# First MLP of blocks 7 and 8 as one pair with seven products, blocks 1 to 6 ordered by the list scheduler

## The chip, the core and the metric

The kernel runs on one core of one Trainium2 chip. Five engines take their instructions each from its own queue, in order: TensorE (PE; its weight loads are listed as PEld), VectorE (DVE), ScalarE (ACT), GpSimd (POOL) and SyncE (SP). Almost all DMAs are issued by SP, a few by ACT. The metric is the device time of one execution in microseconds (us), lower is better.

## The reference

A linear attention is followed by two MLPs over the same 4608 rows. All inputs are float32.

```python
# q, k, v: (8, 8, 576, 64); w_in: (512, 2048); w_out: (2048, 512), for each MLP
q_s = softmax(q, axis=-1);  k_s = softmax(k, axis=2)      # each with its maximum subtracted
kv  = einsum('bhsd,bhse->bhde', k_s, v)
x   = einsum('bhsd,bhde->bhse', q_s, kv)   # then (batch, row, heads*64) -> (4608, 512)
h = x @ w_in;  x = (h * clip(h + 3, 0, 6) / 6) @ w_out    # first MLP
h = x @ w2_in; out = (h / (1 + exp(-h))) @ w2_out         # second MLP
```

## The kernel before

**Tiling.** The 4608 rows are nine blocks of 512 rows (block 0 to 8). A value of float32 is held as two parts, an upper one (the value cast to fp32r) and a lower one (what the cast lost), and each product of two such values is three matmuls: upper by upper, upper by lower, lower by upper. Every large matmul is 128x128 by 128x512.

**A block of an MLP, the plain way.** It has 16 steps f, one for each 128 columns of the hidden layer. `mm1` (L493) makes h of a step by 12 matmuls into one of two PSUM banks `h`. The gate follows: ACT makes r (`relu`, L506), DVE multiplies (`times`, L513), ACT casts the upper part of g (`upper`, L521), DVE makes the lower part (`lower`, L524). `mm2` (L563) adds the step to four PSUM banks y0 to y3 by 12 matmuls. The order written out by hand is mm1 of a step, then mm2 of the step before. After the 16th step, `finish` copies y0 to y3 out, two on DVE and two on ACT, and stores them to DRAM (`yd`). That makes 384 matmuls for a block.

**A pair of blocks by seven products.** `second_mlp` takes two blocks at once. The rows of the pair and the weights are each cut in quarters, and seven products of sums of quarters stand in for eight (Strassen and Winograd). `inner` (L998) is the first matmul of the MLP and `outer` (L1151) the second, with 336 matmuls each: 672 for a pair. `PAIR` names the operands: A11 ... S4 are parts of the weights, B11 ... T4 parts of the rows. The weight parts lie ready made in DRAM (`ws`) and come back by way of a ring of six buffers of 512 KB (`fetch`, L884); two parts lie in one buffer. The row parts of the next pair are made while a pair runs (`x_ahead`, `xd`).

**Stages.** Block 0 of the first MLP is ordered by a list scheduler (`Plan`: jobs with an engine, a duration, a key, what they wait for, and buffers taken and given back). Blocks 1 to 8 of the first MLP run the plain way in a loop written by hand, in which each step also holds a share of the attention of a later block (`k_max` ... `x_mm`, one unit for each pair of heads, 36 units in all, `begin` says at which step a unit starts) and of the weight parts of the second MLP (`Parts`: 16 jobs, each converts two raw rows of weights, makes four sums on POOL, splits them on ACT and DVE through a buffer `sp`, and stores them to `ws` by SP). The attention's q goes through DRAM to be transposed (`q_store`, `q_load`, issued by ACT). In block 8 the row parts of the pair (1, 2) are made (`first_operands`). Then the second MLP runs on the pairs (1, 2), (3, 4), (5, 6), (7, 8), and at last on block 0 the plain way. The transposes back to rows (`turn`, L1191) of a pair run in the pair after it.

**How an instruction waits.** Each engine takes its queue in order; an instruction whose data or buffer isn't there holds up all behind it on that engine, SP's DMAs included.

Of the kernel before, what the change touches and what calls it, by code (L numbers as in the profile page):

```python
# [9 lines left out]
F32 = mybir.dt.float32  # L10
# [8 lines left out]
P = 128  # L19
# [9 lines left out]
def efficient_attention_then_two_mlps(  # L29
# [23 lines left out]
    KVS = NP + 1  # L53

# [48 lines left out]
    class Conv:  # L103
# [68 lines left out]

    class Parts:

        def __init__(self, i, o):
# [8 lines left out]

        def sums(self):
            at = {}
            for c, names in zip(self.conv, self.names):
                for h, name in enumerate(names):
                    at[name] = c.a[:, h * HALF : (h + 1) * HALF]
            self.s = raw.tile([P, 4, HALF], F32, tag="raw", name="ws_sum")  # L190
            for n in range(4):
                at[f"S{n + 1}"] = self.s[:, n]
            for to, x, y, op in (
                ("S1", "A21", "A22", ALU.add), ("S2", "S1", "A11", ALU.subtract),
                ("S3", "A11", "A21", ALU.subtract), ("S4", "A12", "S2", ALU.subtract),
            ):
                nc.gpsimd.tensor_tensor(out=at[to], in0=at[x], in1=at[y], op=op)  # L197

        def upper(self, n):
            s = self.s.rearrange("p n d -> p (n d)")  # L200
            self.src = self.conv[n].a if n < 2 else s[:, (n - 2) * DM : (n - 1) * DM]
# [1243 lines left out]
```

## Time and profile before

| | us |
|---|---|
| median of three runs (1623.17 to 1623.67) | 1623.55 |
| the profiled execution | 1623.47 |
| its span, first to last instruction | 1621.5 |
| PE busy | 1593.3 (98%) |
| first matmul of block 1 to the first of the pair (1, 2) | 752.2 |
| one pair of the second MLP in the steady state | 156.3 |
| block 0 of the second MLP, at the end | 95.4 |

A busy time is the sum of an engine's instructions in a stretch. PE's matmuls are pipelined, so that the shown duration of a row of matmuls is a little longer than the distance between the starts of two rows; the chain of waits shows the distance. The clock column is the granted clock of TensorE as a share of full speed. In a group of instructions "idle before" is the time that the engine had waited ahead of them, and the name behind the arrow is what ended that wait.

### The profile page before, as it was taken

Reading aid. Unit: us, or ns where it says so; the run is one execution under the profiler, and the core shown is the slowest. Engines: PE = TensorE matmul, PEld = TensorE weight load, DVE = VectorE, ACT = ScalarE, POOL = GpSimd, SP = SyncE. Lnnn points to the kernel's source line nnn. Section 1 sums busy time; section 2 is a strip of 40 time slices with the busy share of each in tenths; the row PEclk is TensorE's granted clock in tenths of the full one; section 3 lists DMA queues with packets and bytes.
Section 4 is the critical chain, followed back from the end, with each engine's and each line's share of the span. In section 5 each row is a group of like instructions: output and inputs, shape, how many; then the busy total and the mean of one; then the engine's idle time right before and its main releaser. Section 6 shows DMA issues by size and latency. Waiting matters only on the chain.

```text
span 1621.5 us, 22000 instructions
## 1 busy us (share of the span) xinstructions
PE 1593.3 (98%) x7612; PEld 1302.4 (80%) x7612; DVE 1054.9 (65%) x1785; ACT 747.9 (46%) x1322; POOL 314.3 (19%) x270
## 2 busy tenths in 40 slices
PE   5999999999999999999999999999999999999998
PEld 3777888888888888888888788888888888888887
DVE  8997666666676666665555677767767775567522
ACT  6885444444444444344334445445544553445322
POOL 2101111101111111111122361045104500340000
PEclk8999999999999999999999999999999999999999
DMA  8912444445544545433351898889879996769730
GB/s 259 343 36 69 126 107 144 120 142 147 158 117 118 146 123 150 132 109 110 95 169 52 303 339 299 285 299 356 299 271 313 331 329 243 223 210 364 251 125 26
DMA packets 291837, 317.60 MB, mean 196 GB/s; under 512 B 113424, under 2 KB 197392, under 8 KB 291728
## 3 DMA queue, kind: packets, MB, share of 16 engines
q1 hardware_dynamic: 228768, 300.97, 55.1%
q10 hardware_dynamic: 62960, 15.25, 4.2%
q8 instruction: 60, 0.98, 0.3%
q14 instruction: 49, 0.40, 0.1%
HBM read 234.62 MB, written 81.53 MB: 195 GB/s over the span
## 4 chain that ended last, share of the span: by engine, by line
PE 90%; DVE 5%; DMA 2%; ACT 1%; issue 1%; POOL 0%; SPq 0%; ACTq 0%; DVEq 0%; POOLq 0%
PE h L493 25%; PE y L563 22%; PE pb L1151 19%; PE pb L998 18%; PE y L565 3%; PE pa L451 2%; PE pa L337 1%; DVE fa L132 1%; DVE fa L128 1%; PE pb L1191 1%; DMA yd<-o 0%; DVE fa L121 0%; DVE wi L153 0%; DMA ring<-ws 0%; DMA ws<-sp 0%
## 5 line engine op out<-in xcount | busy, mean ns | idle before, releaser
L493 PE MATMUL h<-x,wi 128*128 128x512 f32 x1920 | 472.7, 394 | 2.3 <-DVE wi L153 1.0
L493 PEld LDWEIGHTS h<-x,wi 128*128 128x128 f32 x1920 | 356.5, 188 | 79.2 <-DVE wi L153 2.8
L563 PE MATMUL y<-g,wo 128*128 128x512 f32 x1728 | 418.1, 391 | 0.0
L563 PEld LDWEIGHTS y<-g,wo 128*128 128x128 f32 x1728 | 322.5, 188 | 68.0
L998 PE MATMUL pb<-xo,ring 128*128 128x512 f32 x1344 | 315.0, 392 | 1.3 <-DVE U L985 1.2
L1151 PE MATMUL pb<-gsp,ring 128*128 128x512 f32 x1344 | 305.9, 389 | 0.0
L1151 PEld LDWEIGHTS pb<-gsp,ring 128*128 128x128 f32 x1344 | 252.3, 188 | 52.3
L998 PEld LDWEIGHTS pb<-xo,ring 128*128 128x128 f32 x1344 | 250.1, 188 | 55.0 <-DVE U L985 1.7
L513 DVE SCALAR_TENSOR_TENSOR r<-r,h 128x512 f32<-128x512 f32 x128 | 87.8, 686 | 197.5 <-ACT r L506 197.2
L985 DVE TENSOR_TENSOR gsp<-g,gsp 128x512 fp32r<-128x512 f32 x192 | 138.1, 725 | 55.0 <-ACT gsp L1087 51.4
L1087 ACT CAST gsp<-g 128x512 fp32r<-128x512 f32 x192 | 117.6, 623 | 106.5 <-DVE gsp L985 76.7
L506 ACT ACTIVATE r<-h 128x512 f32<-128x512 f32 x144 | 86.1, 598 | 147.4 <-PE h L493 126.1
L521 ACT CAST g<-r 128x512 fp32r<-128x512 f32 x144 | 89.5, 621 | 120.0 <-DVE r L513 108.0
L524 DVE TENSOR_TENSOR g<-r,g 128x512 fp32r<-128x512 f32 x144 | 103.8, 721 | 53.5 <-ACT g L521 43.8
L985 POOL TENSOR_TENSOR s<-U,s 128x512 f32<-128x512 f32 x32 | 45.4, 1419 | 324.1 <-DVE U L985 323.1
L398 POOL TENSOR_TENSOR qe<-qe,qs 128x512 f32<-128x512 f32 x36 | 37.6, 1045 | 347.7 <-DVE qs L393 292.9
L985 DVE TENSOR_TENSOR g<-r,pb 128x512 f32<-128x512 f32 x96 | 65.5, 682 | 41.9 <-ACT r L1011 41.9
L1011 ACT ACTIVATE r<-pb 128x512 f32<-128x512 f32 x96 | 57.3, 597 | 61.2 <-DVE pb L985 52.9
L376 POOL TENSOR_TENSOR qe<-qraw,qm 128x512 f32<-128x512 f32 x34 | 35.9, 1057 | 208.1 <-DVE qm L368 143.7
L354 ACT ACTIVATE kv<-pa,rs 64x64 fp32r<-64x64 f32 x56 | 17.3, 308 | 108.2 <-DMA qt<-zd 57.2
L197 POOL TENSOR_TENSOR ws_sum<-fa 128x256 f32<-128x256 f32 x32 | 29.4, 919 | 156.1 <-ACT r L506 88.6
L1011 ACT ACTIVATE r<-s 128x512 f32<-128x512 f32 x32 | 20.2, 633 | 81.4 <-POOL s L985 81.4
(155 smaller groups left out, 1615.4 us busy)
## 6 DMA issues: line engine op xcount, KB each, us to landing
ring<-ws SPq DMA_DIRECT2D x224, 512.0 KB, 5.0
ws<-sp SPq DMA_DIRECT2D x128, 256.0 KB, 2.5
xd<-gsp SPq DMA_DIRECT2D x84, 256.0 KB, 5.6
xo<-xd SPq DMA_DIRECT2D x42, 512.0 KB, 5.5
yd<-o SPq DMA_DIRECT2D x36, 256.0 KB, 2.5
wi_early<-in_moe_w_in_dram SPq DMA_DIRECT2D x16, 512.0 KB, 8.9
wo_early<-in_moe_w_out_dram SPq DMA_DIRECT2D x16, 512.0 KB, 9.5
wi_raw<-in_moe_w_in_dram SPq DMA_DIRECT2D x16, 512.0 KB, 4.3
```

Source lines behind the costliest of these rows:

```text
L493: nc.tensor.matmul(h, w[:, a, c, :], x[:, e, c, :], start=(c == 0 and n == 0), stop=(c == NC - 1 and n == 2),)
L506: nc.scalar.activation(self.r, self.h, AF.Relu, bias=3.0)
L513: nc.vector.scalar_tensor_tensor(out=r, in0=r, scalar=6.0, in1=h, op0=ALU.min, op1=ALU.mult)
L521: nc.scalar.copy(self.g[:, 0], self.r)
L524: nc.vector.tensor_tensor(out=self.g[:, 1], in0=self.r, in1=f32(self.g[:, 0]), op=ALU.subtract)
L563: nc.tensor.matmul(y[c], w[:, a, cs], g[:, e, :], start=st, stop=sp)
L565: nc.tensor.matmul(y[c], g[:, e, cs], w[:, a, :], start=st, stop=sp)
L985: (eng or nc.vector).tensor_tensor(out=out, in0=a, in1=b, op=how)
L998: nc.tensor.matmul(to, ws_[:, a], e[:, c], start=p in ("P1", "P6", "P5") and c == 0 and m == 0, stop=c == 1 and m == 2, skip_group_check=True,
L1011: nc.scalar.activation(r, d[b, n, key], AF.Sigmoid)
L1087: nc.scalar.copy(t[0], source(p, i))
L1151: nc.tensor.matmul(d[b, p][m], w[:, a, m * P : (m + 1) * P], t[e], start=new and i == 0 and k == 0, stop=i == NPR - 1 and k == 2, skip_gro ...
```

## The change

**What is computed how.** The first MLP runs the plain way on blocks 0 to 6 alone. Blocks 7 and 8 become a pair with seven products in `second_mlp`, which now makes five passes: second MLP of (1, 2), first MLP of (7, 8), second MLP of (3, 4), of (5, 6) and of (7, 8). In the pass of the first MLP the gate is a Relu and a minimum, and the sums go to `yd`, not to the transposes.

**Weight parts of the first MLP.** They are made from the weights that are resident in SBUF (`Resident`: 16 jobs more, each with two whole sums and four sums of halves on POOL, two splits, and stores). All splits now write their sums in place, use two buffers `sp`, and store four pieces of 128 KB where two of 256 KB were.

**Far blocks.** x of blocks 4 to 8 is copied to DRAM (`xq`); blocks 4 to 6 load it again before they start, blocks 7 and 8 in `x_ahead`. The attention of blocks 2 to 8 is spread over 96 steps in place of 112 (`begin`).

**Order.** The hand-written loop is gone. `middle` gives all work of blocks 1 to 6 to a `Plan`, with `held` jobs (the four of a gate) that an engine keeps itself free for. `mm2` is cut in two jobs, `finish` in four copies and four stores. `q_store` and `q_load` go from ACT's queue to SP's.

```diff
+    NCL = NB - 2
+    FAR = 4
+    PASSES = ((1, 1), (0, NCL)) + tuple((1, j) for j in range(3, NB, 2))
...
-    ws = dram.tile([2, 4 * NF, P, DM], F32, name="ws")
+    ws = dram.tile([2, 2, 4 * NF, P, DM], F32, name="ws")
+    xq = dram.tile([NB - FAR, NC, P, BLK], F32, name="xq")
...
+    class Split:
+        def upper(self):
+            self.hi = att.tile([P, DM], F32R, tag="sp", bufs=2, name="sp")
+            if self.keep:
+                self.lo = att.tile([P, DM], F32R, tag="sp", bufs=2, name="sp")
+            else:
+                self.lo = self.src().bitcast(F32R)
+            nc.scalar.copy(self.hi, self.src())
+        def lower(self):
+            nc.vector.tensor_tensor(out=self.lo, in0=self.src(), in1=f32(self.hi), op=ALU.subtract)
+        def store(self):
+            for h, name in enumerate(self.names):
+                to = ws[self.ph, self.o, slot(self.o, self.i, name)]
+                for a, t in enumerate((self.hi, self.lo)):
+                    nc.sync.dma_start(
+                        to[:, a * HALF : (a + 1) * HALF], f32(t)[:, h * HALF : (h + 1) * HALF]
+                    )
...
+        def whole(self, n):
+            w = self.flat(n)
+            nc.gpsimd.tensor_tensor(out=self.t[:, n], in0=f32(w[:, 0]), in1=f32(w[:, 1]), op=ALU.add)
...
     def q_store(u):
-        nc.scalar.dma_start(zd[u], live.pop(("z", u)))
+        nc.sync.dma_start(zd[u], live.pop(("z", u)))
...
+        if j >= FAR:
+            t = live["xq", u] = tmp.tile([P, BLK], F32, tag="t2k", name="xq")
+            nc.scalar.copy(t, live.pop(("px", u)))
+            return
...
-            begin[j * NP + pr] = 3 * pr if j == 1 else (j - 1) * NF + 4 * pr - 3
+            n = (j - 2) * NP + pr
+            begin[j * NP + pr] = 3 * pr if j == 1 else NF - 3 + 24 * n // 7
...
+    def middle():
+        plan = Plan(
+            a=2, h=2, g=1, r=1, z=1, qe=0, qT=1, ke=0, mx=2, m1=1, t2k=5, raw=0, sp=2, x=1, wi=0,
+            **{f"y{c}": 0 for c in range(NC)},
+        )
...
+                m = add(
+                    "PE", 0.69, n - 0.5, lambda s=s, c=c: mm1(s, [c]), [xready.get((j, c)), m],
...
+            m2 = add(
+                "PE", 1.82, n + 0.55, lambda s=s: mm2(s, (0, 1)), [g2, last],
...
+        for fn in plan.run(0, 300e3):
+            fn()
...
-            ws[o, 2 * m : 2 * m + 2].rearrange("s p d -> p s d"),
+            ws[PASSES[b][0], o, 2 * m : 2 * m + 2].rearrange("s p d -> p s d"),
...
+                nc.scalar.activation(r, d[b, n, key], AF.Relu, bias=0.5, scale=1.0 / 6.0)
...
+                nc.vector.scalar_tensor_tensor(
+                    out=g, in0=r, scalar=1.0, in1=x, op0=ALU.min, op1=ALU.mult
+                )
...
-                x_ahead(j + 2, 0, t0 + 7.0, 3.0)
-                x_ahead(j + 2, 1, t0 + 28.0, 3.0)
+                x_ahead(b + 1, 0, t0 + (7.0 if b else 9.5), 3.0 if b else 2.8)
+                x_ahead(b + 1, 1, t0 + 28.0, 3.0)
...
-        when(1.95, lambda: (mm2(last), finish(0, NB - 1)))
+        when(1.95, lambda: mm2(last))
+        for c in range(NC):
+            when(3.4 + c, lambda c=c: (finish_copy(NCL - 1, c), finish_store(NCL - 1, c)))
```

**Two places in the order.** In the changed program mm1 is L553, mm2 L625, `times` L573, `lower` L584, the splits' lower parts L223, the copies of y on DVE L644, the stores of weight parts L229, `fetch` L1150.

DVE at the end of a block, before: the last two gates of block 1 and the two copies of its y.

```order
L513 SCALAR_TENSOR_TENSOR r<-r,h 128x512
L466 TENSOR_TENSOR x<-pa,x 128x512
L524 TENSOR_TENSOR g<-r,g 128x512
L207 TENSOR_TENSOR sp<-ws_sum,sp 128x512
L317 TENSOR_TENSOR ke<-kbuf_94,pa 128x2x5x64
L414 STREAM_TRANSPOSE qz<-qe 128x512
L513 SCALAR_TENSOR_TENSOR r<-r,h 128x512
L524 TENSOR_TENSOR g<-r,g 128x512
L580 TENSOR_SCALAR o<-y_1684 128x512
L580 TENSOR_SCALAR o<-y_1686 128x512
```

The same place after, from the last `lower` of block 1 on (16 instructions stand between that step's `times` and this row; fa and fr are weights in conversion, y_1815 is y0 of block 1):

```order
L584 TENSOR_TENSOR g<-r,g 128x512
L345 TENSOR_TENSOR m_2761<-kbuf_94 128x256
L346 TENSOR_TENSOR m_2762<-m_2761 128x128
L347 TENSOR_TENSOR m_2762<-m_2762,kbuf_94 128x128
L644 TENSOR_SCALAR o<-y_1815 128x512
L223 TENSOR_TENSOR fa<-fa,sp 128x512 x2
L573 SCALAR_TENSOR_TENSOR r<-r,h 128x512
L358 TENSOR_REDUCE mx<-pa 128x1
L492 TENSOR_TENSOR qT<-qt,qT 128x512
L584 TENSOR_TENSOR g<-r,g 128x512
L129 TENSOR_SCALAR fa<-fa 128x512
L573 SCALAR_TENSOR_TENSOR r<-r,h 128x512
```

Before, gate and copies follow each other closely; after, conversions, splits and attention stand among them, and the copy of y2 (y_1817) comes 16 rows behind that of y0.

PE at the same place after, between the second half of block 1's last mm2 and the first mm2 of block 2 (y_1815 to y_1818 are block 1's banks, y_2904 block 2's first):

```order
L625 MATMUL y_1818<-g,wo 128x512
L352 MATMUL pa<-ident,m_2762 128x128
L553 MATMUL h<-x,wi 128x512 x12
L364 MATMUL pa<-ident,mx 128x128
L507 MATMUL pa<-qT,kv_93 128x4x48 x3
L507 MATMUL pa<-qT,kv_92 128x4x80 x3
L553 MATMUL h<-x,wi 128x512 x24
L393 MATMUL pa<-vbuf_95,ke 64x65 x10
L625 MATMUL y_2904<-g,wo 128x512
```

Before, one mm1 (12 matmuls of L493) stood there; now three do, 36 matmuls.

SP where the pairs begin, before (block 8's last stores of weight parts, then the ring):

```order
L209 DMA ws<-sp 256x1x256 x6
L92 DMA wo_raw<-in_moe_w_out_dram 128x1024
L209 DMA ws<-sp 256x1x256 x8
L884 DMA ring<-ws 128x2x512 x4
L581 DMA yd<-o 128x512 x4
```

The same place after, its last rows (w_sum is a sum of the first MLP's weights, split in place; xst is x of blocks 7 and 8):

```order
L229 DMA ws<-sp 128x256
L229 DMA ws<-w_sum 128x256
L1150 DMA ring<-ws 128x2x512 x5
L647 DMA yd<-o 128x512
L1150 DMA ring<-ws 128x2x512
L647 DMA yd<-o 128x512 x2
L1430 DMA xst<-xq 128x512 x2
```

Ahead of the first of these rows stand five more pairs of stores of the last job, from fa and from w_sum. The ring's fetches follow the last store of weight parts as before; the splits that these stores wait for now come three in a row behind the last gate (DVE: lower, xo, L223 fa twice, L223 w_sum) with two buffers `sp` for them.

## Rows read from the trace of the kernel before

**Rows 1.** Page, part 1: busy time, share and instructions of each engine

```profile
PE 1593.3 (98%) x7612; PEld 1302.4 (80%) x7612; DVE 1054.9 (65%) x1785; ACT 747.9 (46%) x1322; POOL 314.3 (19%) x270
```

**Rows 2.** Table by stretch: length, busy us (instructions) per engine, clock, DMA share, GB/s

```profile
0.00:32.00 32.00, 16.69 (x116) 10.88 (x116) 26.01 (x70) 18.40 (x34) 9.77 (x18) 0.88 0.90 263
...
242.70:338.00 95.30, 95.30 (x496) 78.05 (x495) 61.24 (x118) 40.85 (x75) 15.86 (x16) 1.00 0.47 135
...
146.90:899.10 752.20, 752.12 (x3757) 617.63 (x3755) 464.42 (x840) 320.03 (x563) 125.35 (x122) 1.00 0.43 126
...
1063.10:1219.40 156.30, 156.30 (x705) 129.31 (x705) 111.33 (x160) 74.87 (x132) 44.94 (x32) 1.00 0.88 310
```

**Rows 3.** Chain that ended last, one piece: start, us, what

```profile
1451.30 74.80 PE pb L1151 x330
```

**Rows 4.** DVE groups, 146.9 to 899.1: busy us, mean ns, idle before, releaser

```profile
L524 DVE TENSOR_TENSOR g<-r,g 128x512 fp32r<-128x512 f32 x128 | 92.7, 724 | 42.5 <-ACT g L521 32.8 <-PE y L563 4.8
L513 DVE SCALAR_TENSOR_TENSOR r<-r,h 128x512 f32<-128x512 f32 x128 | 87.8, 686 | 197.5 <-ACT r L506 197.2
L207 DVE TENSOR_TENSOR sp<-fa,sp 128x512 fp32r<-128x512 f32 x32 | 32.2, 1005 | 3.7 <-ACT sp L203 3.6
L128 DVE CUSTOM_DVE_ANT_0 fa<-fa,fr 128x1024 uint16<-128x1024 uint16 x32 | 24.7, 773 | 4.4
L207 DVE TENSOR_TENSOR sp<-ws_sum,sp 128x512 fp32r<-128x512 f32 x31 | 21.4, 689 | 8.1 <-ACT sp L203 7.9
L317 DVE TENSOR_TENSOR ke<-kbuf,pa 128x640 f32<-128x640 f32 x24 | 19.5, 813 | 1.7 <-PE pa L309 1.7
L466 DVE TENSOR_TENSOR x<-pa,x 128x512 fp32r<-128x512 f32 x28 | 19.1, 683 | 0.0
...
L121 DVE TENSOR_SCALAR fa<-fa 128x512 uint32<-128x512 uint32 x32 | 18.3, 573 | 17.5 <-ACT fa L115 17.5
...
L132 DVE SCALAR_TENSOR_TENSOR fa<-wo_raw,fa 128x512 uint32<-128x512 uint32 x16 | 11.1, 692 | 0.5
...
L580 DVE TENSOR_SCALAR o<-y 128x512 f32<-128x512 f32 x16 | 10.2, 680 | 0.0
...
L345 DVE TENSOR_SCALAR rs<-pa 128x1 f32<-128x1 f32 x24 | 3.6, 148 | 5.5 <-PE pa L337 5.5
```

**Rows 5.** POOL groups, 146.9 to 899.1, same columns

```profile
L398 POOL TENSOR_TENSOR qe<-qe,qs 128x512 f32<-128x512 f32 x27 | 28.2, 1045 | 284.1 <-DVE qs L393 233.3 <-ACT x L461 50.8
...
L197 POOL TENSOR_TENSOR ws_sum<-fa,ws_sum 128x256 f32<-128x256 f32 x16 | 18.6, 1163 | 0.0
L197 POOL TENSOR_TENSOR ws_sum<-ws_sum,fa 128x256 f32<-128x256 f32 x16 | 11.8, 737 | 1.3
```

**Rows 6.** Queue time of DMA issues (timeline: start, us)

```profile
442.55 2.88 ACTq L424 DMA_DIRECT2D qt<-zd  x4
```

**Rows 7.** SP timeline, one store of weight parts: start, us, what

```profile
334.04 1.23 SPq L209 DMA_DIRECT2D ws<-sp  x2
```

**Rows 8.** Page, part 6: KB of one DMA and median us to landing

```profile
ring<-ws SPq DMA_DIRECT2D x224, 512.0 KB, 5.0
ws<-sp SPq DMA_DIRECT2D x128, 256.0 KB, 2.5
```

**Rows 9.** Timeline at the end of block 8: start, us, what, idle before

```profile
889.34 0.62 ACT L203 CAST sp<-fa 128x512 fp32r<-128x512 f32 x1 [1.59 <-DMA ws<-sp]
...
893.91 0.62 ACT L203 CAST sp<-ws_sum 128x512 fp32r<-128x512 f32 x1 [0.49 <-DMA ws<-sp]
...
899.11 2.88 PE L998 MATMUL pb<-xo,ring 128*128 128x512 f32 x12
...
901.50 1.94 SPq L884 DMA_DIRECT2D ring<-ws  x4
...
916.83 0.33 SPq L1121 DMA_DIRECT2D xd<-gsp  x1
...
918.18 6.99 PE L998 MATMUL pb<-xo,ring 128*128 128x512 f32 x28 [1.23 <-DVE U L985]
```

More of the change, by code (lines that the diff above doesn't have):

```diff
@@ L171, in slot, with sums_in_place @@
         )
+    NAMES = ((("A11", "A12"), ("A21", "A22")), (("A11", "A21"), ("A12", "A22")))
+    INTO = {"A22": "S1", "A21": "S3", "A11": "S2", "A12": "S4"}
+    def sums_in_place(o, rows):
+        at = {
+            name: r[:, h * HALF : (h + 1) * HALF]
+            for r, names in zip(rows, NAMES[o]) for h, name in enumerate(names)
+        }
+        return [
+            lambda to=to, x=x, y=y, op=op: nc.gpsimd.tensor_tensor(
+                out=at[to], in0=at[x], in1=at[y], op=op
+            )
+            for to, x, y, op in (
+                ("A22", "A21", "A22", ALU.add), ("A21", "A11", "A21", ALU.subtract),
+                ("A11", "A22", "A11", ALU.subtract), ("A12", "A12", "A11", ALU.subtract),
+            )
+        ]
@@ L199, in upper @@
[L199 to L212 removed]
+            self.conv = [Conv(1, 2 * i + n, o) for n in range(2)]
@@ L550, in gate, with mm2 @@
         g.lower()
-    def mm2(s):
+    def mm2(s, which=range(3)):
         ph, j, f = s
-        if f == 0:
+        if f == 0 and 0 in which:
             acc[ph, j] = [ps_y.tile([P, 512], F32, tag=f"y{c}", name=f"y{c}") for c in range(NC)]
-        g, w, y = gt.pop(s), wo[ph, f], acc[ph, j]
+        g, w, y = gt[s], wo[ph, f], acc[ph, j]
         for n, (a, e) in enumerate(((0, 0), (1, 0), (0, 1))):
+            if n not in which:
+                continue
             for c in range(NC):
@@ L668, in once @@
                 started = False
+                coming = [v for _, v in ready if v in held and at[v] > now + 1e-9]
                 for entry in list(ready):
@@ L672, in once @@
                     if at[i] > now + 1e-9 or busy.get(eng, 0.0) > now + 1e-9:
+                        continue
+                    if i not in held and any(
+                        jobs[v][0] == eng and now + 1e-9 < at[v] < now + us - 0.25
+                        for v in coming
+                    ):
                         continue
@@ L1078, in split_tile @@
                 ]
+            if n == 2:
+                return [
+                    att.tile([P, BLK], F32R, tag="sp", bufs=2, name="gsp") for _ in range(2)
+                ]
             if n < 2:
@@ L1174, in do @@
                     add(one, at, one)
+                done = {"C11": (four, 0, 0), "C12": (two, 0, 1), "C21": (one, 1, 0), "C22": (three, 1, 1)}
+                ph, j = PASSES[b]
+                if not ph and name in done:
+                    x, a, h = done[name]
+                    nc.sync.dma_start(yd[j + h, 2 * a + m], x)
             names = {
@@ L1200, in second_mlp @@
         uses = {}
-        BB = (NB - 1) // 2
-        for b in range(BB):
+        BB = len(PASSES)
+        for b, (ph, j) in enumerate(PASSES):
             t0 = T
@@ L1247, in second_mlp @@
                         )
-                for k in range(2 * NCH):
+                for k in range(2 * NCH if ph else 0):
                     when(T + 3.95 + 5.0 * k, lambda j=j, k=k: turn(j, k))
```

505 lines of the change are left out of this document (311 added, 194 removed), and 3 rows, old and new, of the table new.

## The prediction

> **What bounds the kernel now.** I read the page's busy times first [rows 1]: PE 98%, no other engine over 65%. Then the table by stretch, to see where PE isn't busy [rows 2]. In the first 32.0 us it works 16.7; in the 752.2 us of blocks 1 to 8 it works 752.1, in a steady pass of a pair 156.3 of 156.3. So the time is PE's own work, at a clock of 1.00, and the stages of the change have no stall to recover, but for 1.23 us at the start of the first pair, the last row of its group [rows 9]. Next the price of that work: 330 matmuls take 74.80 us in the chain of waits [rows 3], so one takes 0.2267 us, 12 take 2.72 and a plain step of 24 takes 5.44. Last I read the groups of DVE and POOL in blocks 1 to 8 [rows 4, 5] and the DMA issues [rows 6 to 9], since the change packs their work closer. A matmul that is left out is worth its 0.2267 us in full, if the other engines follow.
>
> **Matmuls.** Two plain blocks have 2 x 384 = 768, a pair 672: 96 fewer, x 0.2267 = **-21.8 us**. The attention's matmuls stay as many; the transposes too (a first-MLP pass has none behind it, four second-MLP pairs have theirs as before).
>
> **Blocks 1 to 6 become denser.** They lose 32 steps, 32 x 5.44 = 174.1 us, and have 752.2 - 174.1 = 578.1. DVE did 464.4 there [rows 2]. It loses 32 gates of 0.686 + 0.724 (45.1), four copies of y at 0.680 (2.7) and eight lower parts of x at 0.683 (5.5), and gains 32 splits at 0.689 to 1.005 (22.0 to 32.2) [rows 4]: 433 to 443 of 578, 75 to 77% where it was 62%. ACT loses 64 instructions of a gate and gains 32 upper parts and 12 of far x, all near 0.62 [rows 9]: 308 of 578, 53%, and is rid of issuing DMAs. POOL gains 32 whole sums at 1.045 (33.4) and 64 sums of halves at 0.737 to 1.163 (47.2 to 74.4) [rows 5]: 125.4 becomes 206 to 233, 36 to 40%. None of them is full, so on average the work is covered by PE; what counts is the places where it is bunched.
>
> **Where it is bunched: the end of block 1.** The order shows it. From the `times` of block 1's step 14 to the `times` of block 2's step 2 DVE has 53 instructions: five `times` and four `lower` (6.33), four conversions of three each (0.573 + 0.773 + 0.692, together 8.15), five splits (two from fa at 1.005, three at 0.689: 4.08), one copy of y, one lower part of x (1.36), and 25 of the attention by the rows of the same view (15 groups, L317 to L345: 9.76). Sum 29.7 us [rows 4]. The `times` of step 2 frees the bank h that mm1 of step 4 takes. From the end of mm1 of step 14 to the start of that mm1, PE has 96 matmuls (21.8) and the attention's matmuls of two units. A unit costs PE (752.1 - 3072 x 0.2267) / 27 = 2.06, so two cost 4.1: 25.9 in all. DVE starts about 0.9 later, behind the `relu`. PE so waits 29.7 + 0.9 - 25.9 = **4.7 us**. If the two dear splits cost 0.689 it is 4.1; every wait of DVE in that row adds to it, and I allow 8. The order already has three mm1 in a row there, all that two banks h, one r and two g can hold, so nothing else hides it. At the end of block 4 the same sum goes from the second `times` of block 5 to DVE's second copy of y: 17 instructions, 10.5 us, plus 0.9, against 36 matmuls, one unit and the two matmuls ahead of y2's (8.2 + 2.06 + 0.45): **0.7 us**. At the other places DVE has over a microsecond in hand.
>
> **The seam to the first pair.** Before, SP issued the ring's four fetches at 901.50, 2.4 us after the first matmul of the pair (899.11), and PE ran on [rows 9]. The third buffer is first read by P7, that is after 12 matmuls, the 12 of the last mm2 and 12 more: 36 x 0.2267 = 8.2 us after the start. A fetch takes 5.0 to land [rows 8]. After, SP comes to the fetches behind the last w_sum store. The far x of the last unit is copied by ACT behind the last x_mm, 0.8 after the start; two splits of fa follow, then that of w_sum, which needs a buffer `sp` back. One round of split, store and landing took 893.91 - 889.34 = 4.6 us with one buffer [rows 9]; ACT can split w_sum at 0.8 + 4.6 = 5.4. Split and lower part take 0.62 + 0.69, the store 1.23 [rows 7]: the fetch is issued near 8.0 and lands near 13.2. PE waits **5 us** at P7. From below 2 (a landing nearer the 2.5 of a store [rows 8]), from above 8 (fa's sums late on POOL: four at 1.163 in place of 0.737, and SP late too). During this wait DVE and ACT catch up, and x of the next pair starts 2.5 units of 1.36 later, so the old 1.23 us goes (**-1.2**).
>
> **SP and the far x.** SP gets 27 times a store and four gathers of q. Four gathers held ACT's queue for 2.88 us [rows 6], so 0.72 each. The issuing time of 384 smaller stores isn't in the trace: from 0.33 for a plain DMA of 256 KB (at 916.83) [rows 9] to 0.62, half of 1.23, for a store of weight parts [rows 7]. I take 0.33, since they are plain two-dimensional pieces like that row, and keep the other end for the range. The gathers add 27 x (0.33 + 2.88) = 87 us, the stores 127 to 238; far x has 20 stores and 12 loads, 11 us at 0.33. That is 225 to 336 on top of loads that SP had already: room in 578, but a late gather holds ACT's queue at the cast of q, and a late store at the next split. Between an mm1 and its own mm2 lie two other halves of a step, 5.44 us, and the gate itself is 0.62 + 0.69 + 0.62 + 0.72: 2.7 us of such lateness are hidden. I put **2 us** on what isn't, 0 to 8. The Trainium skill, "DMA: Bandwidth & Descriptors", section "Issuing engines are not separate DMA queues", says that issuing on several engines only saves the time to initiate a DMA, which is usually small beside the DMA itself. The row of 0.72 for 64 KB doesn't bear out "small"; by the page this term would be 0.
>
> **Sum.** The profiled execution took 1623.47 (span 1621.5 and 2.0 around it), the median is 1623.55. 1623.5 - 21.8 + 4.7 + 0.7 + 5 - 1.2 + 2 = **1613 us**.
>
> **Rivals.** *Full gain:* neither place costs, since the fetches land early and DVE's rows at the end of block 1 are shorter when POOL is idle beside them: 1623.5 - 21.8 - 1.2 = 1600.5, to 1606 with half of one place. For it: PE has been covered without a gap at 62%. Against it: two sums that go by rows. 13%.
>
> *POOL slows DVE:* splits beside sums on POOL took 1.005, away from them 0.689 [rows 4], and POOL's own sums 1.163 against 0.737 [rows 5]. If each of the 160 added POOL instructions costs one DVE instruction 0.32, DVE gets 51 us more, 490 of 578; that is 1.7 instructions a step, 2.2 us more over the four steps at the end of block 1, and 1 us at each of two ends of blocks with 1 to 2 in hand. It gives 1617, up to 1621. Against it: the scheduler keeps the two apart by its port. 15%. The Trainium skill, "SBUF — State Buffer", section "SBUF: two separate sides", says that a DVE instruction with two SBUF inputs and one of GpSimd that reads SBUF exclude each other for the whole instruction. The rows agree that both lengthen, by 0.3 to 0.4 on average and not by a whole instruction; by the rule a DVE instruction could wait up to 1.16.
>
> *SP becomes the bound (slower):* if a store of 128 KB costs SP the 0.72 of a gather, the 384 take 276, and the gathers and their stores 87. With the older loads (27 units of six to seven DMAs and 48 direct stores and 30 loads of weights, all at 0.62: 110 and 48) that makes 521 of 578. If SP also stands 2.5 us [rows 8] at each of 27 units for the q that it has just stored, it is 589, over PE's 578. It decides from there: 11 us, and 5 to 25 more where its bursts fall on ACT's splits. 1613 + 11 to 36 = 1624 to 1649, 1632 in the middle. For it: all is in one queue in order. Against it: a plain DMA showed 0.33, and other DMAs stand between store and gathers. 14%.
>
> *It doesn't do what it says:* the pass of blocks 7 and 8 doesn't run at a pair's 152.3 of matmuls. DMAs are at 0.88 in a pass already [rows 2], and x comes by way of DRAM. It fetches no more than the other passes: 4%, some 1625. Other mishaps, either way, 4%.
>
> **How the numbers follow.** The forecast, 1606 to 1617, has 50%. Two tenths of a per cent, 3.2 us, is about what a measurement of this kernel can tell from no change. Below 1620.3 lie the forecast, the full gain, most of the POOL case and some mishaps: 79%. From 1620.3 to 1626.8: 8%; above: 13%. The range leaves out the best of the full gain and most of the SP case: 1602 to 1625.
>
> **What would show it.** Right: PE 96 matmuls fewer, blocks 1 to 6 in 578 + 5 to 10 us, one PE gap of 4 to 6 us at the first steps of block 2 that ends on DVE, another of about 5 in the first 10 us of the first pair that ends on the ring, passes of 152 to 157 us. Wrong: gaps that end on ACT waiting for q or for a store, spread over all units (SP), or DVE groups near 1 us (POOL), or no gap at all (full gain).

## The result and the profile after

The changed kernel takes **1640.0 us** (median of four runs, 1636.85 to 1645.21), the kernel before took 1623.4 beside it on the same chip: 1.0107 of its time, 95% interval 1.0077 to 1.0138. It is 1.1% slower, clear of the noise, and the time lies outside my range of 1602 to 1625. The profiled execution took 1636.85.

PE does less than before, as planned: 1584.3 us busy against 1593.3 [rows 1]. This is the first part of the page of the changed kernel:

```profile
PE 1584.3 (97%) x7516; PEld 1288.7 (79%) x7516; DVE 1147.1 (70%) x1901; ACT 798.1 (49%) x1422; POOL 457.7 (28%) x398
```

The table by stretch of the changed kernel follows. Its columns are the stretch, its length, the busy time and instructions of PE, PEld, DVE, ACT and POOL, the granted clock, the DMA share and GB/s. The stretches are blocks 1 to 6, the pair (1, 2), the first MLP of (7, 8), and the pairs (3, 4) and (5, 6). It answers to [rows 2].

```profile
146.74:754.87 608.13, 589.10 (x2993) 476.32 (x2992) 448.12 (x795) 298.80 (x535) 224.79 (x218) 0.99 0.70 212
754.87:917.36 162.49, 158.47 (x686) 130.05 (x684) 111.32 (x165) 74.94 (x131) 44.99 (x32) 0.98 0.89 312
917.36:1074.48 157.12, 156.62 (x706) 129.12 (x704) 110.60 (x161) 74.44 (x132) 45.12 (x32) 1.00 0.89 318
1074.48:1226.80 152.32, 152.32 (x674) 126.13 (x672) 110.76 (x161) 70.11 (x124) 45.26 (x32) 1.00 0.88 307
1226.80:1383.09 156.29, 156.29 (x705) 129.27 (x704) 109.70 (x161) 74.75 (x132) 44.85 (x32) 1.00 0.88 309
```

The last three rows are as predicted: the passes run without a gap (but for 0.5 us in that of (7, 8)), at the old price of a matmul (in the chain of waits below, 41.71 / 184 = 0.2267 us, as in [rows 3]). The first row holds most of the loss: 608.1 us where I had 585.5. PE stands still for 19.0 of them, and its busy 589.1 is more than the 578.1 of its matmuls at full clock.

```profile
1308.45 41.71 PE pb L1470 x184
```

What did PE wait for? These are waits in blocks 1 to 6 of the changed kernel (engine, instruction, what it waited for; us in total, times, longest). I show the longest rows in which ACT waits for a DMA, and the longest of PE's own:

```profile
ACT qT L487 <- DMA qt<-zd: 13.4, 6, 4.0
ACT fa L117 <- DMA yd<-o: 13.3, 4, 5.2
ACT sp L220 <- DMA ws<-sp: 13.0, 11, 4.2
...
ACT fa L117 <- DMA wi_raw<-in_moe_w_in_dram: 11.6, 6, 4.5
...
ACT x L671 <- DMA xr<-xq: 6.9, 4, 4.5
...
ACT fa L117 <- DMA wo_raw<-in_moe_w_out_dram: 6.8, 5, 3.9
...
PE y L625 <- DVE g L584: 6.2, 3, 3.1
...
PE h L553 <- DVE r L573: 5.5, 7, 1.7
...
PE y L625 <- ACT g L581: 4.5, 3, 3.3
```

PE never waits for a DMA in these rows, only for the gate's instructions on DVE (`times`, now L573, and `lower`, L584) and ACT (`upper`, L581). But ACT waits for six kinds of DMA, 65 us in these rows, and the gate stands in ACT's queue behind them.

The end of block 1 shows how the chain goes. Timelines of the changed kernel (start, us, instruction, how many; in brackets the idle time ahead and what ended it), first PE, then ACT, then SP's issuing:

```profile
252.32 3.00 PE L625 MATMUL y<-g,wo 128*128 128x512 f32 x8 [3.29 <-ACT g L581]
...
262.90 1.58 PE L625 MATMUL y<-g,wo 128*128 128x512 f32 x4 [3.12 <-DVE g L584]
...
266.41 4.83 PE L553 MATMUL h<-x,wi 128*128 128x512 f32 x12 [1.71 <-DVE r L573]
```

```profile
251.10 0.66 ACT L117 ACTIVATE fa<-wi_raw 128x512 f32<-128x512 f32 x1 [4.52 <-DMA wi_raw<-in_moe_w_in_dram]
251.67 0.60 ACT L581 CAST g<-r 128x512 fp32r<-128x512 f32 x1
```

```profile
240.41 3.18 SPq L480 DMA_DIRECT2D qt<-zd  x4
243.69 1.97 SPq L304 DMA_DIRECT2D vbuf<-in_v_dram  x2
245.75 0.62 SPq L308 DMA_DIRECT2D vbuf<-in_v_dram  x1
246.48 0.54 SPq L102 DMA_DIRECT2D wi_raw<-in_moe_w_in_dram  x1
247.10 2.00 SPq L229 DMA_DIRECT2D ws<-sp  x4
```

Read from below: SP issues four gathers of q and three loads of v, 5.8 us of issuing, and only then, at 246.48, a load of raw weights. It lands near 251.1. ACT has stood 4.52 us at the conversion that needs it (L117), the gate's cast (L581) is the next in its queue, and PE stands 3.29. The two later gaps, 3.12 and 1.71, end on DVE. They are the place of which the prediction spoke.

The last row also gives the disputed price: four stores of 128 KB in a row take SP 2.00, so 0.50 each. These are the stores from `sp` and the gathers of q of blocks 1 to 6 by the instruction (count, shortest, median and longest in ns, first and last start):

```profile
L229 SPq DMA_DIRECT2D ws<-sp x250: 319/444/1982, 160.2 to 751.7; - x125
L480 SPq DMA_DIRECT2D qt<-zd x108: 562/634/1686, 198.8 to 714.3; - x108
```

My choice for a store was 0.33, which is nearly the shortest; the median is 0.44. All rows of SP's issuing in blocks 1 to 6, added, make some 450 us of 608. A row joins DMAs of one kind together with the pauses between them; added by the instruction it is 412, and 196 of 752 before. The jobs of the plan carry durations for SP that add to 294.

### The profile page after: what moved, and what is told of

Its sections match the earlier page's. It is cut to its first block, busy times and chain, and to the rows that moved or that the text cites. A ratio compares the mean times of both kernels' runs of the same rounds, so it can differ in the third digit from the quotient of the medians.

```text
span 1635.1 us, 23181 instructions
## 1 busy us (share of the span) xinstructions
PE 1584.3 (97%) x7516; PEld 1288.7 (79%) x7516; DVE 1147.1 (70%) x1901; ACT 798.1 (49%) x1422; POOL 457.7 (28%) x398
## 4 chain that ended last, share of the span: by engine, by line
PE 78%; DVE 9%; DMA 4%; POOL 2%; issue 2%; ACT 2%; SPq 1%; ACTq 0%; DVEq 0%; POOLq 0%
PE pb L1470 23%; PE pb L1303 21%; PE h L553 15%; PE y L625 13%; PE y L627 3%; DVE fa L140 1%; DVE fa L136 1%; PE pa L507 1%; PE pa L393 1%; DMA ws<-sp 1%; DVE fa L223 1%; POOL w_sum L191 1%; DVE r L573 1%; DVE fa L129 1%; DMA ring<-ws 1%
## 5 line engine op out<-in xcount | busy, mean ns | idle before, releaser
L1303 PE MATMUL pb<-xo,ring 128*128 128x512 f32 x1680 | 393.7, 393 | 4.5 <-DMA ring<-ws 3.2
L553 PE MATMUL h<-x,wi 128*128 128x512 f32 x1536 | 388.9, 399 | 7.9 <-DVE r L573 5.5
L1470 PE MATMUL pb<-gsp,ring 128*128 128x512 f32 x1680 | 382.4, 389 | 0.0
L1303 PEld LDWEIGHTS pb<-xo,ring 128*128 128x128 f32 x1680 | 315.1, 189 | 71.6 <-issue 3.6
L1470 PEld LDWEIGHTS pb<-gsp,ring 128*128 128x128 f32 x1680 | 315.3, 188 | 65.5
L553 PEld LDWEIGHTS h<-x,wi 128*128 128x128 f32 x1536 | 285.5, 191 | 73.9 <-DVE r L573 9.3
L625 PE MATMUL y<-g,wo 128*128 128x512 f32 x1344 | 328.4, 393 | 10.7 <-DVE g L584 6.2
L625 PEld LDWEIGHTS y<-g,wo 128*128 128x128 f32 x1344 | 251.9, 189 | 66.2 <-DVE g L584 7.3
L1405 ACT CAST gsp<-g 128x512 fp32r<-128x512 f32 x240 | 146.9, 623 | 134.6 <-PE pb L1470 67.6
L581 ACT CAST g<-r 128x512 fp32r<-128x512 f32 x112 | 69.4, 620 | 86.5 <-DVE r L573 65.2
L584 DVE TENSOR_TENSOR g<-r,g 128x512 fp32r<-128x512 f32 x112 | 87.7, 783 | 30.8 <-ACT g L581 29.2
L573 DVE SCALAR_TENSOR_TENSOR r<-r,h 128x512 f32<-128x512 f32 x96 | 65.5, 683 | 48.4 <-ACT r L566 47.0
L1290 POOL TENSOR_TENSOR g<-g 128x512 f32<-128x512 f32 x40 | 55.3, 1382 | 63.5 <-DVE g L1290 51.5
L1290 DVE TENSOR_TENSOR U<-pb,s 128x512 f32<-128x512 f32 x80 | 54.8, 684 | 15.7 <-PE pb L1303 13.6
```

The lines of the kernel that those rows point to most:

```text
L553: nc.tensor.matmul(h, w[:, a, c, :], x[:, e, c, :], start=(c == 0 and n == 0), stop=(c == NC - 1 and n == 2),)
L573: nc.vector.scalar_tensor_tensor(out=r, in0=r, scalar=6.0, in1=h, op0=ALU.min, op1=ALU.mult)
L581: nc.scalar.copy(self.g[:, 0], self.r)
L584: nc.vector.tensor_tensor(out=self.g[:, 1], in0=self.r, in1=f32(self.g[:, 0]), op=ALU.subtract)
L625: nc.tensor.matmul(y[c], w[:, a, cs], g[:, e, :], start=st, stop=sp)
L1290: (eng or nc.vector).tensor_tensor(out=out, in0=a, in1=b, op=how)
```

## The experiments

The first runs take one load away each. The later ones build on what those showed. The line numbers of a kernel with an edit are up to 30 higher than those of the changed kernel.

**e2 and e3: SP's work, or the bytes?** e2 leaves the stores of the first MLP's weight parts out (the pass of blocks 7 and 8 reads those of the second MLP in their place). e3 replaces the four gathers of a unit by one plain copy, of as many bytes.

```diff
-                Split(0, o, i, lambda n=n: self.t[:, n], [INTO[x] for x in NAMES[o][n]], False)
+                Silent(0, o, i, lambda n=n: self.t[:, n], [INTO[x] for x in NAMES[o][n]], False)
...
-        for b in range(4):
-            nc.sync.dma_start(
-                t[b * 32 : b * 32 + 32].rearrange("i (c a k) -> i c a k", c=NCH, a=4), zb[b]
-            )
+        nc.sync.dma_start(t, zd[u])
```

> Same order of everything, but the weight parts of the first MLP are not stored (124 stores from the split sums and 48 direct ones, some 86 us of SP's issuing and 40 MB), and the pass of blocks 7 and 8 reads the second MLP's parts in their place, so its output is not the reference's. DVE, ACT, POOL and PE keep all their instructions. Theory SP: blocks 1 to 6 fall from 608 us to 583 to 592, time 1612 to 1622. Rival POOL: 600 to 608 us, since POOL and DVE do the same beside each other.

> Same order; the four gathers that fetch the transposed q are one plain load of the same 256 KB, so x is not the reference's. It takes some 27 x 2.4 = 65 us of issuing from SP and leaves all stores. Theory SP in the form that issuing time is short: blocks 1 to 6 fall from 608 us to 586 to 596. In the form that the added stores crowd the DMA engines: 600 to 608 us, since the bytes stay. Rival POOL: 603 to 608 us.

Blocks 1 to 6 by the table by stretch, of e2 and of e3 (columns as above):

```profile
146.59:743.03 596.44, 587.00 (x2992) 476.90 (x2991) 449.62 (x795) 298.12 (x535) 224.30 (x218) 0.99 0.58 168
```

```profile
147.47:743.96 596.49, 586.93 (x2992) 476.92 (x2991) 447.43 (x795) 298.79 (x535) 224.55 (x218) 0.99 0.68 216
```

Both take 12 us off blocks 1 to 6 and 16 off the whole (1623.9, ratio 1.0001 [0.9991, 1.0010], and 1623.7, 1.0004 [0.9994, 1.0013]). e2 moves less (168 GB/s for 212), e3 as much as the changed kernel (216). What they share is SP's time: 365 and 390 us of issuing for some 450. The q of e3 lands no sooner as one copy (a median of 3.0 us behind its issue, 2.7 for a gather). So it is the issuing. Each gives less than I had expected of SP alone (583 to 592 and 586 to 596 for these blocks).

**e12: both.** What is left when SP has little to do?

> e2 and e3 together, in the order of the changed kernel: no stores of the first MLP's parts and a plain load of q, some 150 us less for SP to issue (x and the pass of blocks 7 and 8 are not the reference's). e2, e3 and e5 each brought blocks 1 to 6 from 608 to 596 or 597 us. Theory: with any one of them SP is no longer late where it matters, and the rest, 18 us over the 578 of the prediction, is in the order itself (gaps that end on DVE at the ends of blocks 1 and 4, and the lower clock after them): 594 to 597 us, time 1620 to 1625. Rival: SP is still late in them, and another 5 to 12 us come: 584 to 592 us.

```profile
147.29:741.24 593.95, 583.89 (x2993) 474.51 (x2991) 449.98 (x795) 298.69 (x535) 224.48 (x218) 0.99 0.54 169
```

With 305 us of issuing blocks 1 to 6 take 594.0, and the whole 1621.6 (0.9992 [0.9983, 1.0001]). From the changed kernel to here is 14.1 us: that is what SP's lateness costs, as far as e12 takes it away (it also moves fewer bytes; e3, which moves them all, gives 11.6). 10.1 us of idle time stay. At the end of block 1 of e12 PE's timeline shows the largest of them:

```profile
258.34 1.29 PE L625 MATMUL y<-g,wo 128*128 128x512 f32 x4 [3.67 <-DVE g L584]
...
261.85 5.00 PE L553 MATMUL h<-x,wi 128*128 128x512 f32 x12 [1.98 <-DVE r L573]
```

With another 0.53 behind them these make 6.2 us. The ends of blocks 4 and 6 add 2.4 and 1.3. ACT still waits for DMAs in e12, once 2.77 us for a load of weights at the end of block 1, so a part of the 10.1 can be SP's; that wasn't separated.

**e4: does POOL slow DVE?** The sums of halves of the first MLP's parts are left out.

```diff
-                lambda m=m: sums_in_place(o, [self.t[:, n] for n in range(2)])[m]() for m in range(4)
+                lambda: None for m in range(4)
```

> Same order; of POOL's added sums the 64 of halves (0.84 us each, 54 us) are left out, so the first MLP's parts are not the right ones and the output is not the reference's; the 32 whole sums, the splits and all stores stay. Theory POOL: blocks 1 to 6 fall from 608 us to 588 to 597, DVE's L584 from 783 ns to under 750. Theory SP: 602 to 608 us.

```profile
147.53:757.29 609.76, 589.27 (x2993) 476.98 (x2992) 435.57 (x795) 297.96 (x535) 168.57 (x154) 0.99 0.71 212
```

POOL has 56 us less, DVE 12.5 less with as many instructions: POOL's sums do lengthen DVE's work. But blocks 1 to 6 are no shorter (609.8), and the whole takes 1637.8 (1.0086 [1.0068, 1.0103]). At the end of block 1 the two waits that end on DVE are 3.12 and 2.01 long here, where the changed kernel has 3.12 and 1.71. The mechanism of that rival exists, and PE doesn't feel it here. Whether it would where SP isn't late wasn't tried.

**e1: the plan with true durations of SP.** The order is made by the list scheduler. Here its durations for SP are those measured in the profile.

```diff
-                n_v[u] = dma(1.0, key(-2.5), lambda: load_v(u), 320, [kvmm[u - 2]])
+                n_v[u] = dma(1.95, key(-2.5), lambda: load_v(u), 320, [kvmm[u - 2]])
...
-                z1 = dma(1.4, key(4), lambda: q_load(u), 256, [z0], ["t2k", "z"])
+                z1 = dma(2.85, key(4), lambda: q_load(u), 256, [z0], ["t2k", "z"])
...
-            st = dma(1.4, key, split.store, 512, [lo], [], sp + list(give))
+            st = dma(2.05, key, split.store, 512, [lo], [], sp + list(give))
```

> Same work; only the durations that the list scheduler takes for SP's DMAs are changed, from its own (0.35 us a store of 128 KB, 1.4 for the four gathers of q, 1.0 for the loads of v ...) to those that the trace of the changed kernel shows (0.51, 2.85, 1.95 ...). SP issued for 453 us in blocks 1 to 6 where the scheduler had counted some 285. Theory SP (its queue runs late against the order, and ACT stands in its own queue at casts whose data SP fetched too late): blocks 1 to 6 fall from 608 us to 582 to 592, and the time to 1612 to 1624. Rival POOL (DVE's two-input instructions lengthen beside POOL's sums): unchanged, 603 to 610 us, time about 1637. Rival DVE bunched at the ends of blocks, as predicted: gaps of 4 to 6 us at the start of block 2 stay.

It missed by far: 1691.6 us, 1.042 [1.0405, 1.0436]. PE's timeline of e1 shows the end of block 1 as good as healed, and one huge gap near the end (two more, of 12.15 at 571 and of 4.97 at 665, end on ACT's copy of y and on its work on far x):

```profile
257.26 2.56 PE L625 MATMUL y<-g,wo 128*128 128x512 f32 x10 [0.71 <-DVE o L644]
...
731.73 0.49 PE L393 MATMUL pa<-vbuf,ke 128*64 128x65 f32 x4 [51.44 <-ACT xq L517]
```

Waits of ACT in e1 between 676 and 735 us:

```profile
ACT sp L220 <- DMA ws<-sp: 17.2, 4, 4.9
```

An order that knows what SP costs avoids the gaps at the end of block 1. It also puts off work by its keys, and at the end ACT's copy of far x (L517) stands behind splits and conversions (L121, 11.3 us more for stores from `fa`) which each wait until a buffer's store has landed. So the changed kernel's order counted on an SP that doesn't exist, and an honest order then seems to lack buffers `sp` and priority for y and far x; e6 gives it all of these.

**e10, e11, e5: a third buffer, less issuing.** e10 gives splits a third buffer `sp` (the room comes from two small tiles). e5 leaves the buffers and lets SP issue less: two pieces of a split go in one DMA where their places in `ws` rise, and DVE writes the transposed q in another order (ACT and DVE read it back accordingly), so that a gather has longer runs. e11 is both.

```diff
-            self.hi = att.tile([P, DM], F32R, tag="sp", bufs=2, name="sp")
+            self.hi = att.tile([P, DM], F32R, tag="sp", bufs=3, name="sp")
```

```diff
+                if at[0] < at[1]:
+                    to = ws[self.ph, self.o, at[0] : at[1] + 1 : at[1] - at[0]]
...
-        zb = zd[u].rearrange("(a i) (c b k) -> b i c a k", a=4, b=4, c=NCH)
+        zb = zd[u].rearrange("(a i) (b q) -> b i a q", a=4, b=4)
```

> The changed kernel with a third buffer sp (m1 and qs have moved into other tiles), so that the scheduler makes another order; SP's durations and all DMAs are as in the changed kernel. Theory SP: SP's queue still runs late against the order, so blocks 1 to 6 take 595 to 610 us and the time (with some 6 us for the place of the tiles) is 1634 to 1650. Rival: the buffers were the cause: 580 to 590 us and 1617 to 1628.

> Order of all engines as in the changed kernel, but SP is given less to issue for the same data: where two pieces of a split go to slots in rising order they are one DMA of 256 KB (56 of the 96 splits), and q lies in DRAM so that the gathers take pieces of 512 B in place of 128 B. By the rows (1.24 us for two pieces of 256 KB against 2.05 for four, a gather near 0.42 against 0.71) that is 45 + 31 = 76 us less. Theory SP: as with the plain load of q, blocks 1 to 6 fall from 608 us to 595 to 599 and the time is 1622 to 1627. If it was not SP's time but the 128 B pieces or the missing stores themselves that counted, less than half of that comes. The gap at the start of block 2 that ends on DVE stays (5 us), and so does the lower clock behind it.

> As e10, and SP has less to issue as in e5 (pieces of 256 KB, q in pieces of 512 B); the scheduler still counts SP by its old durations. Theory SP: the blocks fall by the 12 us that e5 got over the changed kernel, to 583 to 598. The rest to e6's 584 is what counting SP's true durations brings.

Blocks 1 to 6 of e10, of e5 and of e11:

```profile
145.76:757.84 612.08, 588.87 (x2992) 476.24 (x2991) 446.12 (x798) 302.76 (x538) 222.09 (x218) 0.99 0.71 213
```

```profile
146.54:744.15 597.61, 585.72 (x2992) 475.04 (x2991) 447.00 (x795) 298.77 (x535) 224.43 (x218) 0.99 0.68 216
```

```profile
146.49:742.54 596.05, 584.10 (x2993) 474.06 (x2991) 451.09 (x798) 301.48 (x538) 223.38 (x218) 1.00 0.69 219
```

A third buffer alone gains nothing (612.1; 1642.5, 1.0113 [1.0097, 1.0128]). Less issuing, with every byte and every result kept, gains 10.5 us in blocks 1 to 6 without it (1624.9, 1.0012 [1.0002, 1.0021]) and 16.0 with it. In e11 the whole gains less, 1629.1 (1.0033 [1.0022, 1.0044]); the reason, which holds for e10 too, is in the last section. SP's issuing was 382 us in e5. By the instruction, as above, a store of two pieces took a median of 0.39 us there, where a single one took 0.43, and a gather 0.43 for 0.63:

```profile
L230 SPq DMA_DIRECT2D ws<-sp x79: 359/388/1627, 160.0 to 740.1; - x79
...
L491 SPq DMA_DIRECT2D qt<-zd x108: 303/430/708, 197.8 to 702.3; - x108
```

**e6: less issuing, true durations, third buffer.** e6 is e11 with the durations as measured, and with priority for the copies of y and for far x (their keys are lowered by 30).

```diff
-            xc = add("ACT", 0.62, key(6), lambda: x_upper(u), [xm], ["t2k"], ["a"])
+            xc = add("ACT", 0.62, key(6) - 30, lambda: x_upper(u), [xm], ["t2k"], ["a"])
...
-                z1 = dma(1.4, key(4), lambda: q_load(u), 256, [z0], ["t2k", "z"])
+                z1 = dma(1.75, key(4), lambda: q_load(u), 256, [z0], ["t2k", "z"])
```

> As the run before, and the order is made anew: the scheduler counts SP's DMAs with their measured durations, has three buffers sp instead of two (m1 and qs have moved into other tiles), and gives the copies of y and of far x the right of way to a buffer t2k. Theory: what held the work back when SP's durations were counted truly (1691 us) was that buffers sp and t2k are held until a store has landed; with them the gaps at the start of block 2 and at the ends of blocks go too: blocks 1 to 6 in 578 to 588 us, time 1603 to 1614. Rival (DVE is bunched at the end of block 1 whatever the order, 4.7 us and its clock): a gap of 4 to 6 us that ends on DVE at the start of block 2, 594 to 600 us, time 1622 to 1628.

```profile
146.72:731.06 584.34, 579.98 (x2992) 473.58 (x2991) 452.67 (x798) 301.49 (x538) 224.49 (x218) 1.00 0.70 223
```

584.3 us, the size that I had predicted for these blocks (585.5); 4.4 idle, and PE's work 580.0 at a clock of 1.00. The whole is 1616.4 us, 0.9956 [0.9941, 0.9970]: faster than the kernel before. From e11 to e6 is 11.7 us in these blocks. Whether the durations or the priority brings them wasn't separated.

**e7 and e8: the seam.** The ring's four fetches become jobs of the plan, ahead of the last stores; e7 on top of e6, e8 on the changed kernel alone.

```diff
+            prev = dma(
+                0.45, base + 5.0, lambda k=k: ring_fetch(k), 512,
+                [prev, pair_at["r1"]], ["x"] if k == 2 else [],
+            )
...
-        for k in range(2, 6):
-            fetch(k)
```

> As the run before, and the first four fetches of the ring's large tile stand in the order as soon as the last mm1 of block 6 has freed it, no longer behind the last store of weight parts. Theory seam: the gap of 3.2 us in the first pair that ends on the ring goes, and with it the clock of 0.83 in that stretch (20 us at 0.83 are 3.4 us): 4 to 7 us less than the run before. Rival (the gap goes, but the clock does not depend on it): 3 us less.

> The changed kernel with the ring's first four fetches moved alone, as in the run before. Theory seam: the gap of 3.24 us that ends on the ring at 766 goes, the first pair takes 163 to 165 us in place of 168.1, and the time is 1630 to 1636 where the changed kernel had 1637 to 1640. Rival: the stores of weight parts that now stand behind the fetches hold ACT's split of the last sums and the first gates of the pair longer, and the gap comes back there: no difference.

Neither gains: e7 1617.3 (0.9958 [0.9941, 0.9974]), e8 1640.2 (1.0113 [1.0095, 1.0131]). e7 had nothing to gain: in e6 PE doesn't wait for the ring in the first pair at all, only for `s`, 3.2 us in all. The first pair of the changed kernel waited once for the ring (first row below, PE's timeline); in e8 (the two rows in the second fence) that wait is gone, and PE waits for the sums `s` that ACT copies:

```profile
766.44 15.84 PE L1303 MATMUL pb<-xo,ring 128*128 128x512 f32 x57 [3.24 <-DMA ring<-ws]
```

```profile
763.27 12.53 PE L1311 MATMUL pb<-xo,ring 128*128 128x512 f32 x54 [1.78 <-ACT s L1345]
...
777.89 11.43 PE L1311 MATMUL pb<-xo,ring 128*128 128x512 f32 x42 [2.09 <-ACT s L1351]
```

3.24 gone, 3.87 come: the ring only hid that ACT is late as well, the first time behind a split that waits for the landing of a store, the second behind a cast that waits 2.71 us for a load of far x (`xst`). This is ACT's timeline of e8 at the first (the 168.1 us in the expectation isn't the pair's; by the table above it took 162.5, and in e8 162.4):

```profile
762.12 0.62 ACT L220 CAST sp<-w_sum 128x512 fp32r<-128x512 f32 x1 [2.56 <-DMA ws<-sp]
```

**e9: the place of the tiles.** In e6 and e7 the passes had become 1.6 us longer (157.9, 153.9). The row of the outer matmuls in e6, by line (count, shortest, median and longest in ns), and the piece of its chain:

```profile
L1492 PE MATMUL pb<-gsp,ring x88: 388/394/397, 1299.7 to 1319.8; 128*128 128x512 f32 x88
```

```profile
1285.53 64.50 PE pb L1492 x279
```

64.50 / 279 = 0.2312 us for a matmul, not 0.2267. Taking out the two small tiles, to make room for the third buffer, had moved six of the eight places of the tiles `gsp`, which outer reads, from a multiple of 512 bytes in a partition to 448 past one; the other two stayed 256 past one. e9 is e7 with some tiles placed first, so that all begin 256 past one.

```diff
+            att.tile([P, *shape], F32, tag=tag, bufs=bufs, name="place")
```

> As e7, with the tiles of the small pool in another place. In e6 and e7 a pass of a pair takes 1.6 us more (157.9 where 156.3 stood, 153.9 where 152.3): the matmuls of the second half of a pass take 0.2312 us in place of 0.2267. In those two kernels the tiles that these matmuls read begin 448 bytes past a multiple of 512 in a partition; here they begin 256 past one, as some of them did in the changed kernel. If the place matters: 156.3 and 152.3 again, 6 us less than e7, time 1609 to 1612. If it was the third buffer sp or the DMAs: as e7, 1615 to 1618.

```profile
L1500 PE MATMUL pb<-gsp,ring x90: 389/389/389, 1289.8 to 1310.0; 128*128 128x512 f32 x90
```

```profile
1046.81:1199.13 152.32, 152.32 (x673) 126.13 (x672) 110.83 (x161) 69.49 (x124) 45.38 (x32) 1.00 0.89 308
```

The matmul is back at 389 ns, the pass at 152.3, and the whole takes **1610.7 us**, 0.9921 [0.9909, 0.9934]: the fastest version here, 29 us under the changed kernel, with everything computed.

## Why the prediction was wrong

**The misses add up.** The profiled run is 23.9 us over my 1613. Of that 22.6 lie in blocks 1 to 6 (608.1 against 585.5), 0.8 in the first pair (162.5 is 4.6 over what it was, I had 3.8), 0.8 in the pass of (7, 8) (157.1 for 156.3); elsewhere it gains 0.3. The median is another 3.2 above the profiled run.

**Blocks 1 to 6, by cause.** They are 30.0 over their 578.1 us:

| | us | predicted |
|---|---|---|
| lateness of SP (608.1 - 594.0, changed kernel to e12) | 14.1 | 2 (0 to 8) |
| gaps of the order that end on DVE (idle left in e12) | 10.1 | 5.4 |
| longer busy time of PE beside those gaps (583.9 in e12, 580.0 in e6) | 3.9 | none |
| PE at full clock (580.0 in e6, 578.1 worked out) | 1.9 | none |

**The step that failed: SP and the far x.** The mechanism stood in the text, the term was mis-sized by seven: 14.1 for 2, and beyond its bound of 8 (8.9 of the 14.1 is idle time of PE, 19.0 - 10.1; the rest is longer busy time). The price of a store wasn't what failed. I took 0.33, from one row of another size, where the row of the same kind gave the other end, 0.62, and the median measured is 0.44. But by the instruction SP issued some 290 us more than the older loads took before (412 now; 196 before, of which 74 were the old stores of weight parts), inside the 225 to 336 that I had reckoned. What failed is that I treated SP's lateness as something that 2.7 us of slack hides. In the trace it comes in bursts: four gathers and three loads of v are 5.8 us in one queue, and what lies behind them, a load of weights, holds ACT and with it the gate. The order was written by a scheduler to which SP's work was 294 us; in truth it was 412, some 450 with the pauses. I had compared what the engines do with the length of the stretch, and not the durations that the order was made with against the rows.

The Trainium skill, "DMA: Bandwidth & Descriptors", section "Issuing engines are not separate DMA queues", has the time to initiate a DMA as usually small beside the DMA itself. For one DMA the rows don't deny it: a gather takes 0.63 us to issue and lands 2.7 behind its issue. But what is small for one adds up in a queue: e3 has as many bytes, some 60 us less of issuing, and takes 16 us less. Here the measurement decides.

**The rival on SP gave the time, and not by its condition.** 1640 lies in its 1624 to 1649, which had 14%. But it was to decide from 589 us of issuing, over PE's 578. SP had some 450 of 608. A queue in order needs no full load to be the bound: it is enough that what is urgent stands behind what isn't.

**The end of block 1: right place, too small, and near by luck.** Two waits that end on DVE there, 3.12 and 1.71 in the changed kernel and 6.2 in all in e12, for 4.7. The sum was to give DVE 29.7 us of work without a pause. In e12 the stretch from the `times` of block 1's step 14 to that of block 2's step 2 takes 34.1, of which DVE works 27.1 (third number of busy time) and stands 7.0, once 2.37 for ACT's cast of x, which itself waits for the attention's matmuls on PE:

```profile
236.86:270.94 34.08, 27.96 (x150) 21.79 (x148) 27.09 (x54) 18.71 (x35) 12.27 (x13) 0.90 0.57 174
```

So a total too large stood in for waits that I had put at none. At the end of block 4 it is 2.4 for 0.7. The 1.3 at the end of block 6 I overlooked. DVE's total was near: 448 us for 433 to 443.

**The clock: no term at all.** PE's lost time is not over when PE starts again. This is a stretch of 5 us of the changed kernel behind the waits of 3.12 and 1.71; the clock is the number behind POOL's:

```profile
265.00:270.00 5.00, 3.59 (x9) 2.83 (x10) 2.96 (x7) 1.53 (x3) 0.00 (x0) 0.50 0.64 223
```

0.50 is the lower of the two levels, 1.2 of 2.4 GHz. In e5 the same place, with a wait of 3.66, has rows of 0.63, 0.50 and 0.85:

```profile
255.00:260.00 5.00, 1.81 (x4) 1.38 (x5) 4.70 (x10) 2.45 (x5) 1.91 (x3) 0.63 0.67 184
260.00:265.00 5.00, 3.78 (x10) 2.65 (x9) 3.26 (x7) 1.54 (x3) 0.00 (x0) 0.50 0.99 346
265.00:270.00 5.00, 5.00 (x24) 4.13 (x23) 3.77 (x7) 3.87 (x8) 0.00 (x0) 0.85 0.38 108
```

The lower clock costs only while PE is busy: 0.37 x 1.81 + 0.50 x 3.78 + 0.15 x 5.00 = 3.3 us. So a wait of 3.7 us cost about 7. In all of blocks 1 to 6 PE was busy 5.7 us longer in e5 than in e6 (585.7 - 580.0), and in the changed kernel 9.1 (589.1 - 580.0), of which 5.2 go with SP's lateness (589.1 - 583.9 of e12; they are within the 14.1) and 3.9 with the gaps of the order. The same sum over stretches of 1 us puts 5.8 of the 9.1 down to the clock, 2.4 of the 3.9, and nothing in e6; what the rest comes from, no run here separates. The Trainium skill, "TensorE: Matmul & The Clock Gate", section "HAM oscillation — how this bites in real kernels", tells of a kernel in which TensorE falls back to half rate in waits for a DMA and starts the next piece of work cold; these rows agree, though the waits end on DVE and ACT.

**The seam: about right in sum.** A gap at P7 that ends on the ring was there, 3.24 for 5; the pair is 4.6 us longer for 3.8. Both pieces of the chain were nearly equally late: e8 shows that the one hides the other.

**Right:** the 96 matmuls and their price (passes of 152.3 to 157.1); the change does what it says; POOL isn't the cause of the loss to SP (e4). The forecast of 585.5 for blocks 1 to 6 can be reached, as e6 shows with 584.3, but not with the order that the change made.

## What to carry to other kernels

An order made by a scheduler is as good as its durations: hold each of them against a row of the trace, DMA issuing first, and ask of a queue in order not only how full it is but what urgent thing stands behind its longest burst. Count a wait of TensorE of several microseconds about double where the rows behind it show the granted clock at half. And when a wait goes by an edit, look for the next late thing at the same place before you book the gain.

## What was unexpected of the hardware

**Where a matmul's moving operand begins in a partition** set its price: 0.2312 us with six of eight places at 448 bytes past a multiple of 512, 0.2267 with all at 256 past (e6 against e9, only the places of tiles changed between e7 and e9: 6.6 us of 1617). In the changed kernel, at 0.2267 too, the six were at a multiple of 512. The same 0.2312 is behind the small gain of e11 in the whole, and in e10, whose tiles lay as in e6. Only these places were tried; why it is so stays open.

**A short wait left the clock alone in one run and lowered it in another.** In e11 four waits, of 0.62, 1.09, 1.33 and 1.93 us between 361 and 376, left the granted clock at 1.00 (the row of the longest, and the stretch of 5 us that holds its end). In e10 a wait of 1.65, with one of 0.28 behind it, was followed by 3 us at 0.50 (the second pair of rows):

```profile
375.55 2.11 PE L647 MATMUL y<-g,wo 128*128 128x512 f32 x8 [1.93 <-ACT g L603]
...
375.00:380.00 5.00, 4.45 (x20) 3.68 (x21) 3.87 (x7) 3.88 (x7) 0.18 (x1) 1.00 0.35 86
```

```profile
521.94 0.44 PE L508 MATMUL pa<-qT,kv 128*128 128x384 f32 x1 [1.65 <-ACT qT L488]
...
523.00:526.00 3.00, 3.00 (x10) 2.61 (x10) 1.56 (x4) 2.21 (x5) 0.00 (x0) 0.50 0.87 292
```

So the length of a wait alone didn't decide it; what did, no run here shows.

**Issuing a DMA held SP longer for 64 KB than for 128 KB.** By the instruction a gather of 64 KB took 0.63 us (median), a store of 128 KB 0.44. With longer runs a gather took 0.43, and two stores in one DMA, 256 KB, 0.39. What it is that SP works through there, no run shows; longer runs made a gather shorter, and one DMA for two pieces took no longer than one for a single piece.
